# Adding a skip term at PSUM eviction instead of by identity matmuls, and a changed instruction-fetch estimate in a kernel's own ordering pass

## The chip, the cores and the metric

The kernel runs on one core of a Trainium2 chip. The core has five engines that run side by side: TensorE (PE, matrix multiplies; its weight loads are shown apart as PEld), VectorE (DVE), ScalarE (ACT), GpSimd (POOL) and SyncE (SP, which only issues DMAs here). Matmuls read SBUF and write PSUM, which has eight banks; DVE and ACT move results from PSUM to SBUF. The metric is the device time of one execution, in microseconds; lower is better.

## The reference, cut to what matters

The kernel computes a forward pass and all its gradients for a block of a state-space layer (a long convolution, done by FFT) times a gated linear unit, behind one layer norm. S is 2048, D is 512, F is 1376, everything is bfloat16.

```python
def _layernorm(x, axis=-1, eps=1e-5):
    m = jnp.mean(x, axis=axis, keepdims=True)
    v = jnp.var(x, axis=axis, keepdims=True)
    return (x - m) / jnp.sqrt(v + eps)
...
    def _B_ref(x, w_gate, w_up, w_down):
        g = jnp.einsum("bsd,df->bsf", x, w_gate)
        u = jnp.einsum("bsd,df->bsf", x, w_up)
        h = _sigmoid(g) * u
        return jnp.einsum("bsf,fd->bsd", h, w_down)
    x = A_q
    xn = _layernorm(x, axis=-1)
    s = _A_ref(xn, A_k, A_v, A_shift_k, A_ssm_k, A_ssm_D)
    g = _silu(_B_ref(xn, B_w_gate, B_w_up, B_w_down))
    return x + s * g
...
    _out, _vjp = jax.vjp(_f, A_q, A_k, A_v, A_shift_k, A_ssm_k, A_ssm_D, B_w_gate, B_w_up, B_w_down)
    _grads = _vjp(grad_out)
```

Inside `_A_ref`, with xn for q: k is shifted by a short convolution and multiplied by v; the result is convolved along S with `ssm_k` by FFT of length 4096; y is that convolution plus `kv * ssm_D`, and s is `q * y`. The gradient of xn has three parts: through the gate path (dg times w_gate transposed), through the up path (du times w_up transposed), and one that comes past both, straight from `q * y`. The third is the skip term of this document; the kernel calls it `dxa`.

## The kernel before

The kernel does not emit instructions as its Python runs. It records every operation (class `Rec`), and at the end `order` puts them in an order, `emit` writes it out. So every matmul of a burst has line 558 in the profile and every other operation line 560, and it is read by engine, operation and tile shape.

`order` is a list scheduler. It keeps a time at which each engine is free, gives each operation an estimated duration (`cost`, `dcost` for DMAs), chooses PSUM banks, and for an operation recorded by `evac` chooses ACT or DVE. Among the operations that are ready on an engine it takes the lowest number, that is, the one recorded earliest. Its inner function `fetch` (line 386) counts PE instructions, two for each matmul (a weight load and the matmul), in blocks of `IBLK` = 256, and makes PE wait until `IFETCH` = 5.0 us have passed since the last block was begun. If that wait is over 0.3 us for a burst of small array tiles (any mode but "full"), a full-array burst is taken in its place, when one is ready (lines 436 to 439). Line 391 adds nothing: both branches of it are 0.0.

The recorded order comes from generators ("streams") that `run_streams` interleaves. Each has a total of work and a start and end on a common scale, the pair of numbers behind its work; the stream whose place on the scale is lowest goes next. The program has three stages, run as such:

- First stage (to about 190 us): the gate and up projections (`strG`) beside the FFTs of the kernel and of kv (`strK`, `strV`).
- Second stage, `stepB`: eight pairs of token blocks q. For each, `d_gen(q)` (44 matmuls of 256 columns: dg and du), `z_gen(q+1)` (22 matmuls of 512 columns, then eight of 128 for a transposition) and `x_gen(q)` (two tiles t, each one identity matmul and 22 matmuls of 512 columns). In `x_gen` the identity matmul (line 1163) puts `dxa[:, t]` into PSUM; the other 22 accumulate on it. ACT copies the sum to SBUF as `dxn` with a row sum (line 1171), DVE multiplies it with xn with a second row sum (1172), and a short chain through `sm` and `u1` gives the norm's gradient.
- Last stage: `dW` (the three weight gradients, 688 full-array matmuls of up to 512 columns), `frontC` (forward FFT of the upstream gradient, small array tiles of 64x128 and 64x32) and `endC` with `backC` and `taps` (inverse FFTs, tiles of 32x128, 64x64 and 128x32, and the short convolution's gradients). `dW` reads transposed blocks L that SP loads by DMA_TRANSPOSE (`ld_L`, twelve of them, three buffers), `backC` reads spectra KK from DRAM (`ld_KK`). `rec.late` (line 1420) marks the first operation recorded after the second stage's buffers are freed.

What sets the order around the change: PE's, DVE's, ACT's and SP's queues as `order` wrote them, and the stream numbers of lines 1409, 1422 and 1423.

Of the kernel before, what the change touches and what calls it, by code (L numbers as in the profile page):

```python
# [8 lines left out]
ACT = mybir.ActivationFunctionType  # L9
ALU = mybir.AluOpType  # L10
# [14 lines left out]
NFB = 11  # L25
# [137 lines left out]
class Rec:  # L163
# [3 lines left out]

    NEAR = 300
    BUBBLE = 0.12
    IBLK, IFETCH = 256, 5.0  # L170
    late = 1 << 30
    ENGS = ("tensor", "vector", "scalar", "gpsimd", "sync")
    KINDS = {"f4": [(0, 1, 2, 3), (4, 5, 6, 7)], "m2": [(4, 5), (6, 7), (2, 3), (0, 1)],
# [178 lines left out]
    def order(self):  # L352
# [28 lines left out]
        pipe = {"gpsimd": 0.0, "hw": 0.0, "act": 0.0}  # L381
        table = None
        pemode = "full"
        iblk = [0, 0.0]

        def fetch(op, t, occ, commit):
            n = 2 * (len(op.alts[0][2]) if op.alts[0][1] == "burst" else 1)
            k, b = iblk
            wait = 0.0
            if k + n >= self.IBLK:  # L390
                gap = self.IFETCH + (0.0 if op.n >= self.late else 0.0)
                wait = max(0.0, b + gap - (t + occ * (self.IBLK - k) / n))
                b = t + wait + occ * (self.IBLK - k) / n
                k -= self.IBLK
            if commit:
                iblk[:] = [k + n, b]
            return wait
        held = [None] * 8
        seq = []
# [23 lines left out]
        while ndone < len(ops):  # L423
# [29 lines left out]
            t, n, e, shared = best  # L453
            op = ops[n]
# [28 lines left out]
            if op.dma:  # L483
                occ, d = self.dcost(alt)
                me = {"gpsimd": "gpsimd", "scalar": "act"}.get(e, "hw")
                t = max(t, pipe[me] - (30.0 if me == "gpsimd" else 12.0))
# [77 lines left out]
def run_streams(streams, until=None):  # L564

    live = [list(st) + [0.0] * (5 - len(st)) for st in streams]
    while live:
        if until is not None and until():
            break
        for st in sorted(live, key=lambda s: s[2] + (s[3] - s[2]) * s[4] / s[1]):  # L570
            try:
                c = next(st[0])
            except StopIteration:
                live.remove(st)
                break
            if c:
                st[4] += c
                break
        else:
            raise RuntimeError("all streams blocked")  # L580
    return live
# [68 lines left out]
def kernel_impl(ctx, tc, A_q, A_k, A_v, A_shift_k, A_ssm_k, A_ssm_D, B_x, B_w_gate, B_w_up, B_w_down,  # L650
                grad_out, out_0, out_1, out_2, out_3, out_4, out_5, out_6, out_7, out_8, out_9):
    nc = tc.nc
# [29 lines left out]
    ident = Ring(ar, [P]).ap  # L682
# [31 lines left out]
    flags = set()  # L714
# [186 lines left out]
    B = ar.view(B_r.blks[0][0], [2, 2, 32, 2 * 32], bf16).rearrange("p g c j (u w) -> p g c j u w", u=2)  # L901
# [173 lines left out]
    for src, w, wT in ((B_w_gate, wg, wgT), (B_w_up, wu, wuT)):  # L1075
        nc.sync.dma_start_transpose(wT[:, 0:NFB - 1, :], src[:, 0:128 * (NFB - 1)])
        ps = nc.ps("m1", [4, 128], f32)
# [79 lines left out]
    def x_gen(q):  # L1157
        dgT, duT, dxa, goj = T[q]["dg"], T[q]["du"], T[q]["dxa"], T[q]["go"]
        for t in range(2):
            i = 2 * q + t  # L1160
            xn = xnA[:, i, :]
            ps = nc.ps("m1", [D], f32)
            nc.burst("full", 0.216, [("matmul", (ps[:], ident, dxa[:, t]), dict(start=True, stop=False))])
            for srcT, wT, last in ((dgT, wgT, False), (duT, wuT, True)):
                for f0, f1 in ((0, 4), (4, 8), (8, 11)):
                    nc.burst("full", (f1 - f0) * 0.216, [("matmul", (ps[:], srcT[:, fb, 128 * t:128 * t + 128], wT[:, fb, :]),
                             dict(start=False, stop=last and fb == NFB - 1)) for fb in range(f0, f1)])
                    yield (f1 - f0) * 512
            dxn, u1, sm = dxn_r.next(), u1_r.next(), small.next()
            r = rstd_all[:, i:i + 1]  # L1170
            nc.scalar.activation(dxn, ps[:], ACT.Identity, accum_out=sm[:, 0:1])
            nc.vector.scalar_tensor_tensor(u1, dxn, 1.0, xn, ALU.mult, ALU.mult, accum_out=sm[:, 1:2])
            nc.vector.scalar_tensor_tensor(sm[:, 2:4], sm[:, 0:2], -1.0 / D, r.to_broadcast([P, 2]), ALU.mult, ALU.mult)
            nc.scalar.activation(u1, dxn, ACT.Identity, bias=sm[:, 2:3], scale=r)
            nc.vector.scalar_tensor_tensor(u1, xn, sm[:, 3:4], u1, ALU.mult, ALU.add)
            nc.vector.tensor_tensor(goj[:, t], u1, goj[:, t], ALU.add)
        dma2o(nc.sync, o1C[:, :, 2 * q:2 * q + 2, :], goj)
# [45 lines left out]
    def dW():  # L1223
        for n, (s, c) in enumerate(jobs):
            f0, w = CH[s][c]
            while ("L", n) not in stC:
                yield 0
            blk = stC.pop(("L", n))
            L = blk.ap
            nblk = -(-w // 128) if s == 0 else 4  # L1230
            for b in range(nblk):
                acc = nc.ps("hi", [512], f32)
                kf = min(128, w - b * 128) if s == 0 else 128
                wo = D if s == 0 else w
                for j0 in range(0, NJ, 2):
                    calls = []
                    for j in (j0, j0 + 1):
                        kw = dict(start=(j == 0), stop=(j == NJ - 1))
                        if s == 0:
                            calls.append(("matmul", (acc[0:kf, :], L[:, j, b * 128:b * 128 + kf], dzA[:, j, :]), kw))  # L1240
                        else:
                            calls.append(("matmul", (acc[:, 0:w], xnA[:, j, b * 128:(b + 1) * 128], L[:, j, 0:w]), kw))
                    nc.burst("full", 2 * (wo / 2400 + 0.0025), calls)
                    if j0 % 4 == 2 and j0 < 14:
                        yield 4 * wo
                ot = ot_r.next()
                nc.evac(ot[0:kf, 0:wo], acc[0:kf, 0:wo], wo)
                if s == 0:
                    nc.sync.dma_start(out_9[f0 + b * 128:f0 + b * 128 + kf, :], ot[0:kf, :])
                else:  # L1250
                    nc.sync.dma_start((out_7 if s == 1 else out_8)[b * 128:(b + 1) * 128, f0:f0 + w], ot[:, 0:w])
                if b == nblk - 1:
                    Lfree.append(blk)
                    ld_L()
                    if n == 3:
                        stC["v"] = ar.view(dz_r.blks[0][0], [NJ, D], bf16)
                        for j in range(0, NJ, 4):
                            dma2(nc.sync, stC["v"][:, j:j + 4], vC[:, :, j:j + 4])
                yield 4 * wo
# [10 lines left out]
    def frontC():  # L1270
        for n in range(8):
            cg, u = n // 2, n % 2
            c0 = cg * GW + 64 * u
            if u == 0:
                yield from step1n(lambda j: y2A[:, j, c0:c0 + GW])
            U = flip(stA["V"][:, 32 * u:32 * u + 32])
            while stC["nY"] + len(YS_r.aps) <= n:
                yield 0
            Y = YS_r.next()
            step3(U, Y)  # L1280
            stC["Y", n] = Y
            yield 2048
# [82 lines left out]
    def endC():  # L1365
        yield from backC()
        row4, row6 = ot_r.next(), ot_r.next()[:, 0:GW]
        for lag in range(4):
            nc.vector.tensor_copy(skout[:, :, lag:lag + 1], res[:, :, 3 - lag:4 - lag])
        po = nc.ps("m1", [GW, 4], f32)  # L1370
        for t in range(4):
            nc.tensor.matmul(po[0:4, :, t], skout[:, :, t], ident, start=True, stop=True)
        nc.evac(row4[0:4, :], po[0:4].rearrange("p a t -> p (a t)"), 512)
        nc.sync.dma_start(out_4.rearrange("(g p) t -> g (p t)", p=P), row4[0:4, :])
        pd = nc.ps("m1", [GW], f32)
        nc.tensor.matmul(pd[0:4, :], dDo, ident, start=True, stop=True)
        for e in range(2):
            nc.evac(row6[0:4].rearrange("p (u w e) -> p e u w", u=2, e=2)[:, e],
                    pd[0:4].rearrange("p (e u w) -> p e u w", e=2, u=2)[:, e], 64)
        nc.sync.dma_start(out_6.rearrange("(g p) -> g p", p=P), row6[0:4, :])  # L1380

    def gated(g, flag):
        yield from g
        flags.add(flag)
    live = run_streams([(gated(stepB(), "B"), 8 * 45056, 0.0, 1.0)], until=lambda: "d5" in flags)
# [5 lines left out]
    live = run_streams(live, until=lambda: "z15" in flags)  # L1391
# [5 lines left out]
    live = run_streams(live, until=lambda: "d7" in flags)  # L1397
# [8 lines left out]
        ld_KK(m)  # L1406
    YS_r = Ring(ar, [2, 1024], n=2)
    V_r, U_r = Ring(ar, [64, 32, 2]), Ring(ar, [32, 32, 2], n=2)
    live = run_streams(live + [(dW(), 35 * 8192, 0.98, 1.79), (frontC(), 8 * 4096, 0.88, 1.38)], until=lambda: "B" in flags)
    for r in [wgT_r, wuT_r, go_r, dg_r, du_r, dxa_r, dxn_r, u1_r]:  # L1410
        r.free()
    kh = Ring(ar, [NJ + 3, D]).ap
# [6 lines left out]
    dm_r = Ring(ar, [4, 32], f32)  # L1419
    rec.late = len(rec.ops)  # L1420
    dw, fr = live
    live = run_streams([(dw[0], dw[1] - dw[4], 0.0, 1.0), (fr[0], fr[1], -0.02, 0.57, fr[4]),
                        (gated(endC(), "back"), 4 * 20480, -0.03, 0.54)], until=lambda: "back" in flags)
    run_streams(live)
    rec.emit()

# [59 lines left out]
```

## Time and profile before

| | us |
|---|---|
| median of 3 runs | 520.48 (520.48 to 520.87) |
| the profiled execution's own time | 521.04 |
| its span, first to last instruction | 519.3 |
| PE busy | 468.8 (90%) |
| DVE busy | 387.1 (75%) |
| ACT busy | 283.1 (55%) |
| POOL busy | 47.6 (9%) |
| mean granted TensorE clock | 0.975 |
| DMA traffic | 111.23 MB, 214 GB/s |

The profiled execution took 521.04 us, of which 1.74 us lie around the span of 519.3. It was 0.56 us above the median. PE is busy almost without a gap from 188 us to 368 us; after that, to 498 us, it has gaps. Busy times of matmuls overlap each other, so a busy PE is not PE at its peak: where PE's pace matters, count how many matmuls go by in a stretch and divide. "issue" in a wait means that the profile shows nothing that the engine waited for.

### The profile page before, as it was taken

The numbers are of one execution on the slowest core, as the hardware profiler recorded it, in microseconds if no ns is written. First come the engines' busy times: TensorE is split into PE (matmuls) and PEld (weight loads), VectorE is DVE, ScalarE is ACT, GpSimd is POOL, SyncE is SP. The second block draws the span as 40 slices with busy tenths as digits, with TensorE's granted clock in tenths as the row PEclk, the third lists the DMA queues.
The fourth block names the chain that finished last, engine by engine and source line by source line (L and its number), as shares of the span: only waits on it lengthen the run. The fifth ranks groups of instructions, "written<-read, shape, count | busy, mean of one in ns | idle before, by whom it ended". The sixth has DMA issues, their size and how long they took to land.

```text
span 519.3 us, 14659 instructions
## 1 busy us (share of the span) xinstructions
PE 468.8 (90%) x6388; PEld 303.4 (58%) x6417; DVE 387.1 (75%) x622; ACT 283.1 (55%) x361; POOL 47.6 (9%) x83
## 2 busy tenths in 40 slices
PE   3899898999899789999999999999867979978995
PEld 3687666777676464556556556444434546646664
DVE  8569988767787895877878778576781699963880
ACT  5557787766875743544454446746653764344111
POOL 5023232121121000000000001000000000000000
PEclk9999999999989999999999999999998989979999
DMA  8998697754849969875865947999999996937866
GB/s 218 252 306 207 232 233 207 215 199 172 264 137 265 224 181 281 245 190 159 249 162 178 256 136 181 234 278 261 280 187 222 247 281 149 235 92 174 176 201 202
DMA packets 162360, 111.23 MB, mean 214 GB/s; under 512 B 102389, under 2 KB 145369, under 8 KB 162296
## 3 DMA queue, kind: packets, MB, share of 16 engines
q1 hardware_dynamic: 154104, 86.49, 68.9%
q0 software_dynamic: 6080, 22.75, 13.0%
q10 hardware_dynamic: 2112, 1.05, 0.8%
q8 instruction: 50, 0.82, 0.6%
q14 instruction: 14, 0.11, 0.1%
HBM read 38.44 MB, written 46.83 MB: 164 GB/s over the span
## 4 chain that ended last, share of the span: by engine, by line
PE 59%; issue 15%; DVE 11%; ACT 7%; DMA 5%; SPq 2%; POOL 0%; DVEq 0%; POOLq 0%; ACTq 0%
PE psum L558 59%; DVE slab L560 11%; ACT slab L560 7%; DMA slab<-slab 2%; SPq L560 2%; DMA slab<-in_A_q_dram 1%; DMA slab<-in_A_v_dram 1%; PE psum L560 0%; POOL slab L560 0%; DVEq L560 0%; POOLq L560 0%; ACTq L560 0%
## 5 line engine op out<-in xcount | busy, mean ns | idle before, releaser
L558 PE MATMUL psum<-slab 32*128 32x64 bf16 (+10 forms) x6379 | 467.1, 260 | 45.0 <-ACT slab L560 18.8
L558 PEld LDWEIGHTS <-slab 128*128 128x128 bf16 (+5 forms) x6408 | 302.7, 102 | 208.8 <-issue 64.7
L560 ACT CAST slab<-psum 128x1024 bf16<-128x1024 f32 (+5 forms) x265 | 221.0, 887 | 162.8 <-PE psum L558 133.3
L560 DVE TENSOR_TENSOR slab<-slab 128x1024 bf16<-128x1024 bf16 (+5 forms) x327 | 242.4, 790 | 42.1 <-PE psum L558 23.4
L560 ACT ACTIVATE slab<-psum 128x1024 bf16<-128x1024 f32 (+2 forms) x60 | 49.8, 835 | 63.1 <-PE psum L558 60.3
L560 DVE CAST slab<-psum 128x1024 bf16<-128x1024 f32 (+3 forms) x27 | 31.0, 1149 | 43.5 <-PE psum L558 23.8
L560 DVE STREAM_TRANSPOSE slab<-slab 128x512 f32<-128x512 f32 x48 | 31.0, 685 | 6.1 <-ACT slab L560 6.0
L560 DVE TENSOR_TENSOR slab<-psum,slab 128x1024 bf16<-128x1024 f32 (+2 forms) x28 | 28.1, 1003 | 8.1 <-PE psum L558 7.5
L560 DVE SCALAR_TENSOR_TENSOR slab<-slab 128x512 bf16<-128x512 bf16 (+1 forms) x48 | 24.8, 528 | 11.3 <-ACT slab L560 11.1
L560 DVE TENSOR_SCALAR slab<-slab 128x1 f32<-128x1 f32 (+9 forms) x63 | 20.5, 364 | 4.1 <-PE psum L558 1.8
L560 POOL DMA_DIRECT2D slab<-slab x8 | 4.3, 541 | 176.6 <-DVE slab L560 176.6
L560 ACT ACTIVATE slab<-slab 128x512 bf16<-128x512 bf16 (+2 forms) x18 | 15.7, 872 | 2.6 <-DVE slab L560 1.3
L560 POOL MEMSET slab<- 128x128 bf16 (+3 forms) x7 | 3.3, 480 | 148.0 <-PE psum L558 144.9
L560 POOL DMA_DIRECT2D KK_d<-slab x16 | 9.0, 563 | 67.1 <-ACT slab L560 52.7
L560 POOL TENSOR_TENSOR slab<-slab 128x1 f32<-128x1 f32 (+1 forms) x20 | 11.3, 574 | 24.9 <-DVE slab L560 22.8
L560 DVE BATCH_NORM_STATS2 slab<-slab 128x6 f32<-128x512 bf16 x16 | 10.5, 672 | 0.8 <-DMA slab<-in_A_q_dram 0.8
L560 POOL DMA_DIRECT2D hS_d<-slab x8 | 8.8, 1097 | 12.7 <-DVE slab L560 6.3
L560 DVE COPY slab<-slab 128x1216 bf16<-128x1216 bf16 (+2 forms) x16 | 7.1, 465 | 0.7 <-ACT slab L560 0.7
L560 POOL DMA_DIRECT2D sF_d<-slab x6 | 3.3, 555 | 10.8 <-ACT slab L560 10.8
L560 ACT ACT_TABLE_LOAD x2 | 2.6, 1283 | 2.9 <-issue 2.9
L560 ACT ACTIVATION_READ_ACCUMULATOR slab<-psum 128x1 f32 x16 | 3.1, 196 | 0.0
L560 POOL DMA_DIRECT2D ksh_d<-slab x4 | 2.2, 562 | 6.7 <-ACT slab L560 6.7
(16 smaller groups left out, 15.8 us busy)
## 6 DMA issues: line engine op xcount, KB each, us to landing
KK_d<-slab POOLq DMA_DIRECT2D x16, 512.0 KB, 5.0
slab<-KK_d SPq DMA_DIRECT2D x16, 512.0 KB, 5.2
out_dram<-slab SPq DMA_DIRECT2D x58, 128.0 KB, 2.9
hS_d<-slab POOLq DMA_DIRECT2D x8, 704.0 KB, 6.2
dgS_d<-slab SPq DMA_DIRECT2D x8, 704.0 KB, 4.1
duS_d<-slab SPq DMA_DIRECT2D x8, 704.0 KB, 7.0
sF_d<-slab POOLq DMA_DIRECT2D x6, 704.0 KB, 4.4
slab<-sF_d SPq DMA_DIRECT2D x6, 704.0 KB, 8.1
```

The lines of the kernel that those rows point to most:

```text
L558: getattr(self.nc.tensor, m)(*[place(v) for v in aa], **{x: place(v) for x, v in kk.items()})
L560: getattr(getattr(self.nc, eng), meth)(*[place(v) for v in a], **{x: place(v) for x, v in k.items()})
```

## The change

There are two edits and the numbers that go with the second.

In `x_gen` the identity matmul is left out, so the first of the 22 matmuls starts the accumulation. ACT's copy with a row sum is replaced by one DVE operation that reads PSUM, adds `dxa[:, t]`, writes `dxn` and gives the same row sum.

In `order`, `IFETCH` becomes a pair. For operations from `rec.late` on, when a new block is begun, the gap to the next one is taken as 6.0 us if the estimated end of the queue of hardware DMAs lies more than 3 us behind the block's begin, else as 4.2 us; before `rec.late` it stays 5.0. The numbers of the three last-stage streams change too: both streams that begin beside the second stage, and `frontC` and `endC` after it.

```diff
-    IBLK, IFETCH = 256, 5.0
+    IBLK, IFETCH = 256, (4.2, 6.0)
...
-        iblk = [0, 0.0]
+        iblk = [0, 0.0, self.IFETCH[0]]
...
-            k, b = iblk
+            k, b, gap = iblk
             wait = 0.0
             if k + n >= self.IBLK:
-                gap = self.IFETCH + (0.0 if op.n >= self.late else 0.0)
                 wait = max(0.0, b + gap - (t + occ * (self.IBLK - k) / n))
                 b = t + wait + occ * (self.IBLK - k) / n
                 k -= self.IBLK
+                gap = 5.0 if op.n < self.late else self.IFETCH[pipe["hw"] > b + 3.0]
             if commit:
-                iblk[:] = [k + n, b]
+                iblk[:] = [k + n, b, gap]
...
-            nc.burst("full", 0.216, [("matmul", (ps[:], ident, dxa[:, t]), dict(start=True, stop=False))])
...
-                             dict(start=False, stop=last and fb == NFB - 1)) for fb in range(f0, f1)])
+                             dict(start=not last and fb == 0, stop=last and fb == NFB - 1)) for fb in range(f0, f1)])
...
-            nc.scalar.activation(dxn, ps[:], ACT.Identity, accum_out=sm[:, 0:1])
+            nc.vector.scalar_tensor_tensor(dxn, ps[:], 1.0, dxa[:, t], ALU.mult, ALU.add, accum_out=sm[:, 0:1])
...
-    live = run_streams(live + [(dW(), 35 * 8192, 0.98, 1.79), (frontC(), 8 * 4096, 0.88, 1.38)], until=lambda: "B" in flags)
+    live = run_streams(live + [(dW(), 35 * 8192, 0.93, 1.64), (frontC(), 8 * 4096, 0.87, 1.54)], until=lambda: "B" in flags)
...
-    live = run_streams([(dw[0], dw[1] - dw[4], 0.0, 1.0), (fr[0], fr[1], -0.02, 0.57, fr[4]),
-                        (gated(endC(), "back"), 4 * 20480, -0.03, 0.54)], until=lambda: "back" in flags)
+    live = run_streams([(dw[0], dw[1] - dw[4], 0.0, 1.0), (fr[0], fr[1], -0.09, 0.53, fr[4]),
+                        (gated(endC(), "back"), 4 * 20480, 0.0, 0.63)], until=lambda: "back" in flags)
```

The built program has 6401 matmuls instead of 6417. Its order is the same up to the first `x_gen`; in the second stage it differs by the edit alone, and from the stage's last pair on every queue is in another order.

## The prediction

> **What bounds the kernel now.** I read the page's busy times first, then the chain of work that ended last, then PE's timeline and busy times by stretch. In the second stage the chain is PE alone:
>
> ```profile
> PE 468.8 (90%) x6388; PEld 303.4 (58%) x6417; DVE 387.1 (75%) x622; ACT 283.1 (55%) x361; POOL 47.6 (9%) x83
> ...
> 202.92 10.74 PE psum L558 x49
> ...
> 213.71 9.08 PE psum L558 x69
> ...
> 222.85 10.74 PE psum L558 x49
> ```
>
> One pair q takes 19.93 us (202.92 to 222.85), all of it PE. The busy times of such a period, and of 8 us in it that hold only 512-column matmuls (columns: stretch, its length, then busy us and count of PE, PEld, DVE, ACT, POOL, the granted clock, DMA share, GB/s):
>
> ```profile
> 231.10:250.90 19.80, 19.70 (x119) 11.35 (x120) 16.07 (x30) 9.51 (x14) 0.00 (x0) 1.00 0.69 198
> 247.50:255.50 8.00, 7.95 (x37) 3.60 (x37) 7.63 (x13) 3.33 (x5) 0.00 (x0) 1.00 1.02 297
> ```
>
> 37 matmuls in 8.00 us are 0.216 us each; DVE has 3.7 us free in a period, ACT 10.3. In the last stage PE has gaps (PE's timeline; in brackets the idle time before a row and what ended it):
>
> ```profile
> 371.11 1.01 PE L558 MATMUL psum<-slab 32*128 32x64 bf16 x72 [1.43 <-DVE slab L560]
> ...
> 387.56 4.66 PE L558 MATMUL psum<-slab 128*128 128x512 bf16 x104 [3.03 <-issue]
> ...
> 400.68 16.22 PE L558 MATMUL psum<-slab 64*64 64x128 bf16 x270 [3.63 <-issue]
> ...
> 420.96 22.28 PE L558 MATMUL psum<-slab 128*32 128x128 bf16 x382 [2.28 <-DVE slab L560]
> ...
> 458.56 1.26 PE L558 MATMUL psum<-slab 32*128 32x64 bf16 x125 [1.85 <-DVE slab L560]
> 461.27 7.62 PE L558 MATMUL psum<-slab 128*128 128x320 bf16 x122 [1.45 <-ACT slab L560]
> ```
>
> With 0.66, 0.46, 0.52, 0.83 and 0.90 (issue) more in the same view, waits for DVE or ACT cost 9.5 us and "issue" 7.6. From 498 us to its end at 514.0 PE runs leftover dW matmuls; then one eviction and the last stores fill the span to 519.3. So every us that PE saves or loses anywhere after 190 us moves the end by one us.
>
> **Identity matmuls: -3.5 us.** 16 x 0.216, in a stage where nothing else sets the pace. ACT loses 0.600 us and the 0.196 of reading its sum for each tile, DVE gains one operation. Rows of the nearest kinds:
>
> ```profile
> L560 DVE SCALAR_TENSOR_TENSOR slab<-slab 128x512 bf16<-128x512 bf16 x32 | 22.4, 717 | 11.2 <-ACT slab L560 11.1
> L560 DVE TENSOR_TENSOR slab<-psum,slab 128x768 bf16<-128x768 f32 x8 | 7.6, 952 | 4.2 <-PE psum L558 4.2
> L560 DVE CAST slab<-psum 128x512 bf16<-128x512 f32 x1 | 0.7, 690 | 0.1
> ```
>
> The trace has no such operation on PSUM: from below 0.69 (the copy), from above 0.95 (two operands, but 768 columns), plus 0.08 for reading the sum. I take 0.83 with it, by the same operation in SBUF. Two a period make DVE 16.07 + 1.66 = 17.7 us busy in a period of 19.93 - 0.43 = 19.50. That is hidden as long as DVE's chain fits. Walked from the end of z's matmuls: hT (1.6) and nine products end at 7.6, the first tile's sum is ready on PE at 4.8, so its eviction waits for nothing; the second tile ends on PE at 10.0 and DVE comes to it at 10.6. Queued behind it are the product with xn, dg and du of the same pair, and 1-sig of the next; dg and du are done by about 17.7, and the next x_gen needs them at 19.5. The transposition needs z's chain after 37 matmuls (8.0 us) and has it at about 5. The tile's PSUM bank is held until 8.4 instead of 5.6 us, and two evictions later PE asks for banks at 10.0. So cost zero, cover 1.8 us a period; were the cover gone, each us over is paid seven times.
>
> **Last stage, waits for DVE and ACT: -4.1.** I laid the orders of the two built programs side by side. For each PE instruction that waits for DVE or ACT I set the PE work since the matmul that feeds the awaited operation against that engine's operations in the same stretch, at the rows' durations. In the old order the tap matmuls have 2.72 us of PE work against 4.98 on DVE, short by 2.26: the trace shows 2.28. All shortfalls of the old order add to 5.8 where the trace has 9.5; those of the new one to 3.3 (1.4 at a 32x128 burst early on, 1.0 at another, four small ones; the tap matmuls no longer wait). Scaled alike, 5.4. Bounds: -6.2 unscaled, 0 if backlog on DVE comes back elsewhere. SP's queue moves too: the eight loads of v, two KK loads and a ksh load now stand right behind a DMA_TRANSPOSE; at 0.55 us an issue after its 9.8 us, v lands some 20 us later, and PE has 18.6 us of work and several fetch waits before it needs it. KK loads have 16 us or more. POOL's few halo copies (0.54 us each) have 16 us and more as well. I give these no cost; the bound above holds it.
>
> **Last stage, instruction fetch: +4.7.** The page lists queue "q8 instruction: 50, 0.82" (packets, MB): 16 KB each, against 12,847 PE instructions, so one packet for 256. The three "issue" gaps lie before PE's instructions 8644, 9156 and 11972, which are 2 and 11 times 256 apart. In the trace a packet starts 0.4 to 4.6 us after PE enters the block before, takes 1 us, and PE goes on no sooner than 1.45 us after it has landed. From one entry to the next it took 7.2 us (380.3 to 387.6) and 6.6 (394.1 to 400.7) while a DMA_TRANSPOSE ran, 4.6 without (470.3 to 474.9). Now the work in each block: 0.216 us for 512 columns, 0.150 for 352, 0.62 for a burst of 64 small 32x128 tiles, 1.0 for 64 of 64x64 or 128x32. The old order's shortest are 2.3, 2.5, 2.6, 3.1, 3.3 and 3.3 us, several covered by other waits. The new one has seven blocks under 4.4: 3.8, 2.9, 3.5 (4.4 with its 1.0 wait), 4.3, 3.4, 1.8, 3.8, together 24.4 us, one run of four of them beside two transposes that now follow each other on SP. At a mean price p of 5.2 (two of seven at 6.5, the others between 3.6 and 5.5) they take 36.4, so 12.0 us of waiting, 12.3 with one small wait near the end; less 7.6 is 4.7. Bounds: p = 4.0 gives 3.9, thus -3.7; p = 6.5 gives 21.1, thus +13.5.
>
> [...]
>
> **Last stage, half clock: -2.5.** Gaps cost twice (busy times as above):
>
> ```profile
> 384.49:387.90 3.41, 0.38 (x3) 0.21 (x3) 3.38 (x6) 1.17 (x2) 0.00 (x0) 1.00 1.29 167
> 387.90:391.31 3.41, 3.41 (x48) 1.29 (x49) 0.64 (x2) 0.00 (x0) 0.00 (x0) 0.50 0.98 236
> ...
> 456.17:459.58 3.41, 1.56 (x130) 1.19 (x129) 2.62 (x6) 2.01 (x3) 0.00 (x0) 1.00 0.10 27
> 459.58:463.00 3.42, 1.97 (x31) 1.18 (x19) 3.35 (x5) 3.42 (x4) 0.00 (x0) 0.50 0.68 161
> ```
>
> After a 3.41-us stretch with PE idle for half or more, the next runs at clock 0.50. The last stage has five such stretches, each worth up to 1.7 us: 8.5. The new order's waits fall mostly on short blocks, where slow work hides under the next fetch; I count four stretches, one of them half hidden: 6.0. Bounds -5 and +3.4. [...]
>
> **Sum.** -3.5 - 4.1 + 4.7 - 2.5 = -5.4. The profiled execution's span 519.3 becomes 513.9, with the 1.74 around it 515.6; that execution was 0.56 above the median: 515.1, I say 515.
>
> **Rivals.**
> 1. Only the matmuls pay, the rest cancels: 517.0. For it: the work in the last stage is the same, and what fetch loses is about what DVE gains. Against: the shortfalls reproduced the old trace's largest wait to 0.02 us. It needs the three last-stage terms to add to about 0.
> 2. Slower, by starved fetch: four short blocks in a row under two transposes. With p = 6.5 the term is +13.5, the sum +3.4, so 524. It decides from p = 6.0 on, where the sum crosses zero (7 x 6.0 - 24.4 + 0.3 = 17.9, less 7.6 is 10.3, against -10.1). For it: two observed blocks at 6.6 and 7.2. Against: both had a transpose in flight over the whole block, and only two or three of the seven do.
> 3. DVE becomes the second stage's bound: if the new operation costs 0.95 + 0.08 and its waits for ACT open another 1.5 us, each of seven periods grows by some 0.6: +4.2, so 519. Against: 1.8 us of cover.
> 4. Fetch stays hidden, each next block there in time: -3.5 - 4.1 - 2.5, no gain from the 7.6 counted, 510.4; with that too, lower still. Against it stand the short blocks. [...]
>
> **How the numbers follow.** The forecast 0.52, rivals 0.20, 0.17, 0.06, 0.05. A change under 0.2% (1.04 us) can't be told from none here. Faster takes the forecast, most of rival 1 and all of 4: 0.75. Same takes the edges of 1 and 3, 0.07; slower 0.18, rival 2 and a little of 3. The likeliest case alone spans 510 to 518; reaching rival 4's edge and into the lighter half of rival 2, 509.5 to 521.5.
>
> **What would show it.** In the changed profile the period should be 19.5 us with DVE near 17.7 busy and PE without gaps to about 360; the new DVE row near 0.75. The tap matmuls' 2.28 should be gone. "issue" gaps should sit at short blocks beside transposes and add to about 12 us, with four half-clock stretches. A period over 19.6, gaps for DVE over 8 us, or "issue" over 18 us would make it wrong.

## The result, and the profile after

Timed together, the changed kernel took 523.89 us (520.39 to 529.26, 20 runs) and the kernel before 519.34 (518.17 to 521.88, 20 runs). The ratio is 1.0088, interval 1.0065 to 1.011: about 4.6 us slower. The forecast was 515.0 with a range up to 521.5. The profiled execution took 526.38 us, its span is 524.6. Where some executions of a kernel took over 1.5% more than its fastest, the ratios below leave these out.

The second stage came out as forecast. From the page of after (busy times; then a group of instructions: busy us, mean ns of one, idle time before):

```profile
PE 466.6 (89%) x6401; PEld 301.7 (58%) x6401; DVE 397.5 (76%) x656; ACT 272.7 (52%) x327; POOL 47.2 (9%) x83
...
L560 DVE SCALAR_TENSOR_TENSOR slab<-psum,slab 128x512 bf16<-128x512 f32 x16 | 11.0, 690 | 5.2 <-PE psum L558 5.2
```

One period in after, busy times by stretch (columns as before: stretch, length, busy us and count of PE, PEld, DVE, ACT, POOL, clock, DMA share, GB/s):

```profile
211.30:230.70 19.40, 19.40 (x120) 11.15 (x118) 17.18 (x34) 8.12 (x11) 0.00 (x0) 1.00 0.65 188
```

The new operation takes 0.69 us, and PE has no gap. The loss lies behind the stage. PE's timeline of after (start, length; in brackets the idle time before the row and what ended it):

```profile
366.69 8.21 PE L558 MATMUL psum<-slab 128*128 128x512 bf16 x116 [3.44 <-ACT slab L560]
...
378.27 11.87 PE L558 MATMUL psum<-slab 64*64 64x64 bf16 x198 [1.20 <-issue]
...
393.68 9.04 PE L558 MATMUL psum<-slab 128*128 128x352 bf16 x234 [2.04 <-DVE slab L560]
405.01 5.03 PE L558 MATMUL psum<-slab 64*64 64x64 bf16 x128 [2.29 <-issue]
411.75 3.91 PE L558 MATMUL psum<-slab 64*64 64x128 bf16 x48 [1.71 <-issue]
...
422.87 12.42 PE L558 MATMUL psum<-slab 32*128 32x64 bf16 x149 [1.41 <-issue]
...
450.94 8.60 PE L558 MATMUL psum<-slab 32*128 32x64 bf16 x281 [1.53 <-DVE slab L560]
462.17 10.27 PE L558 MATMUL psum<-slab 32*128 32x64 bf16 x211 [2.63 <-issue]
```

The first tap matmuls' wait of 2.28 us is gone, as forecast; the second ones now wait 0.80 (at 436.09). But counting every gap of 0.3 us or more after 340 us, waits for DVE and ACT add to 12.15 us (before: 9.48) and "issue" to 10.39 (before: 7.56). DVE itself waits for loads more than it did. Before had one such row:

```profile
347.40 3.88 DVE L560 TENSOR_TENSOR slab<-slab 128x2048 bf16<-128x2048 bf16 x5 [3.14 <-DMA slab<-KK_d]
```

After has four, 7.93 us in all (the one not shown, of 1.08 us for KK, is at 348.01). DVE's timeline of after:

```profile
365.39 6.04 DVE L560 TENSOR_TENSOR slab<-slab 128x2048 bf16<-128x2048 bf16 x9 [2.10 <-DMA slab<-KK_d]
...
394.89 7.42 DVE L560 TENSOR_TENSOR slab<-slab 128x2048 bf16<-128x2048 bf16 x10 [1.26 <-DMA slab<-KK_d]
...
417.15 1.23 DVE L560 TENSOR_TENSOR slab<-slab 128x2048 bf16<-128x2048 bf16 x1 [3.49 <-DMA slab<-KK_d]
```

ACT's timeline of after, just ahead of PE's largest gap:

```profile
366.06 4.93 ACT L560 CAST slab<-psum 128x512 bf16<-128x512 f32 x6 [2.12 <-DMA out_dram<-slab]
```

ACT can't copy a dW bank out because the store that empties its buffer has not landed, so PE gets no bank and waits 3.44 us. (ACT had such a wait in before too, of 3.31 us at 455.97.) SP's queue of after at that place (start, time the issue took):

```profile
355.02 0.54 SPq L560 DMA_DIRECT2D slab<-KK_d  x1
356.99 2.21 SPq L560 DMA_DIRECT2D out_dram<-slab  x3
359.76 10.78 SPq L560 DMA_TRANSPOSE slab<-dgS_d  x1
370.63 1.18 SPq L560 DMA_DIRECT2D slab<-in_A_k_dram  x2
371.90 0.54 SPq L560 DMA_DIRECT2D slab<-KK_d  x1
...
382.92 6.54 SPq L560 DMA_TRANSPOSE slab<-dgS_d  x1
389.55 1.00 SPq L560 DMA_DIRECT2D slab<-KK_d  x2
```

The stores were issued just ahead of a DMA_TRANSPOSE and landed at about 366, some 8.5 us later (their median on the page is 3.5). KK loads are late in two ways. The one issued at 355.02 stood ahead of the DMA_TRANSPOSE and took 10.3 us to land, at 365.37, where DVE waited for it. The one issued at 389.55 stood behind a DMA_TRANSPOSE, went out as soon as SP was free and took 5.2 us; DVE waited until 394.89. The third wait shown, 3.49 us, is put down to KK by the profile, but it is for v: the operation is the taps' product with v, it waits for the semaphores of all eight loads of v, and the last of these, issued at 407.57 behind the next DMA_TRANSPOSE, landed at 417.03. So KK makes 4.44 us of the 7.93 and v 3.49. In the last stage four stretches of 3.41 us ran at half clock, as counted; two of them:

```profile
394.55:397.96 3.41, 3.41 (x65) 1.96 (x51) 3.04 (x4) 2.84 (x3) 0.00 (x0) 0.50 1.17 196
404.79:408.20 3.41, 3.19 (x33) 1.55 (x34) 1.37 (x3) 2.02 (x2) 0.00 (x0) 0.50 1.09 305
```

Last, PE ends at 517.05 and the span at 524.6: 7.6 us of tail, where before had 513.99 and 5.3. The first stage, the same program, ended 1.77 us later than in the profile of before (189.53 against 187.76; the other profiles here, k1's aside, have 187.9 to 189.4), which is the run and not the change.

### The profile page after: what moved, and what is told of

It reads as the page before. It is cut to its first block, busy times and chain, and to the rows that moved or that the text cites. A ratio compares the mean times of both kernels' runs of the same rounds, so it can differ in the third digit from the quotient of the medians.

```text
span 524.6 us, 14678 instructions
## 1 busy us (share of the span) xinstructions
PE 466.6 (89%) x6401; PEld 301.7 (58%) x6401; DVE 397.5 (76%) x656; ACT 272.7 (52%) x327; POOL 47.2 (9%) x83
## 2 busy tenths in 40 slices
DMA packets 162360, 111.23 MB, mean 212 GB/s; under 512 B 102389, under 2 KB 145369, under 8 KB 162296
## 3 DMA queue, kind: packets, MB, share of 16 engines
q1 hardware_dynamic: 154104, 86.49, 70.3%
## 4 chain that ended last, share of the span: by engine, by line
PE 53%; issue 16%; DVE 13%; ACT 8%; DMA 7%; SPq 1%; POOL 0%; DVEq 0%; ACTq 0%; POOLq 0%
PE psum L558 53%; DVE slab L560 13%; ACT slab L560 8%; DMA slab<-in_A_v_dram 2%; DMA out_dram<-slab 2%; DMA slab<-in_A_q_dram 2%; SPq L560 1%; DMA slab<-slab 1%; DMA slab<-KK_d 1%; PE psum L560 0%; POOL slab L560 0%; ACT L560 0%; DVEq L560 0%; ACTq L560 0%; POOLq L560 0%
## 5 line engine op out<-in xcount | busy, mean ns | idle before, releaser
L560 ACT CAST slab<-psum 128x1024 bf16<-128x1024 f32 (+6 forms) x263 | 220.4, 889 | 193.9 <-PE psum L558 172.1
L560 ACT ACTIVATE slab<-psum 128x1024 bf16<-128x1024 f32 (+2 forms) x44 | 40.2, 917 | 40.1 <-PE psum L558 37.2
L560 DVE SCALAR_TENSOR_TENSOR slab<-psum,slab 128x512 bf16<-128x512 f32 x16 | 11.0, 690 | 5.2 <-PE psum L558 5.2
```

The source lines that it names most:

```text
L560: getattr(getattr(self.nc, eng), meth)(*[place(v) for v in a], **{x: place(v) for x, v in k.items()})
```

## The experiments

All ratios are to the kernel before, timed in the same job; 1% is 5.2 us. To change one thing and keep every queue's order, the kernels got a field `sub`: the operation is ordered as it was, and something else is written out in its place.

```diff
-                eng, meth, a, k = op.alts[q]
+                eng, meth, a, k = op.alts[q] if op.sub is None else op.sub
```

### Edit or order?

p1 keeps the order of before and makes the eviction edit; p2 does so with a one-column matmul in the place of each identity matmul. p3 keeps the order of after and puts the identity matmul and ACT's copy back. e1 makes the eviction edit in the source of before and lets the order be laid anew by the old rule and numbers.

```diff
 # p1, in x_gen of before
-            nc.burst("full", 0.216, [("matmul", (ps[:], ident, dxa[:, t]), dict(start=True, stop=False))])
+            nc.burst("full", 0.216, [("matmul", (ps[:], ident, dxa[:, t]), dict(start=True, stop=False))]).sub = ("tensor", "burst", [], {})
...
-            nc.scalar.activation(dxn, ps[:], ACT.Identity, accum_out=sm[:, 0:1])
+            nc.scalar.activation(dxn, ps[:], ACT.Identity, accum_out=sm[:, 0:1]).sub = (
+                "vector", "scalar_tensor_tensor", (dxn, ps[:], 1.0, dxa[:, t], ALU.mult, ALU.add), dict(accum_out=sm[:, 0:1]))
```

```diff
 # p2, in the place of the empty burst
+                "tensor", "burst", [("matmul", (ps[:, 0:1], ident, dxa[:, t, 0:1]), dict(start=True, stop=True))], {})
 # p3, in x_gen of after
+                    skip = [("matmul", (ps[:], ident, dxa[:, t]), dict(start=True, stop=False))] if not last and f0 == 0 else []
+                    nc.burst("full", (f1 - f0) * 0.216, mms(not last)).sub = ("tensor", "burst", skip + mms(False), {})
...
+            nc.vector.scalar_tensor_tensor(dxn, ps[:], 1.0, dxa[:, t], ALU.mult, ALU.add, accum_out=sm[:, 0:1]).sub = (
+                "scalar", "activation", (dxn, ps[:], ACT.Identity), dict(accum_out=sm[:, 0:1]))
 # e1, in x_gen of before
-            nc.burst("full", 0.216, [("matmul", (ps[:], ident, dxa[:, t]), dict(start=True, stop=False))])
...
-            nc.scalar.activation(dxn, ps[:], ACT.Identity, accum_out=sm[:, 0:1])
+            nc.vector.scalar_tensor_tensor(dxn, ps[:], 1.0, dxa[:, t], ALU.mult, ALU.add, accum_out=sm[:, 0:1])
```

> The order of the kernel before, operation by operation, with the eviction edit alone: the 16 identity matmuls are left out where they stood and the DVE operation stands where ACT's copy stood. Theory 1 (the eviction gains, the new last-stage order loses): 16 x 0.216 us, so 3.5 us faster than before, 515.8, give or take 1.5 because all later fetch blocks begin 32 instructions earlier in the work; second-stage period 19.5 us. Theory 2 (the DVE eviction itself costs, by its bank held longer or by DVE's backlog): no faster than before, up to 4 us slower, with PE gaps for DVE in the second stage.

> As p1, but in the place of each identity matmul stands one of a single column, which the next matmul overwrites, so that every later instruction stands in the same place of its fetch block as in the kernel before. Theory 1: 16 x (0.216 - 0.06) gained, 2.5 us faster than before, 516.8. If p1 is off by more than 1.5 us from its forecast and p2 is not, the place of the blocks' boundaries is what made the difference. Theory 2: as p1.

> The order of the changed kernel, operation by operation, with the identity matmul put back before each tile's first matmul and ACT's copy in the place of the DVE operation. Theory 1: the new order alone, so 3.5 us slower than the changed kernel: 8 us slower than before, 527. Theory 2: the order costs nothing, 519 to 520, as before.

> The eviction edit in the source alone; the ordering pass keeps its fetch gap of 5.0 us and the old stream numbers, and makes a last-stage order of its own, which is neither the old nor the new one. Theory 1: second stage 3.5 us shorter, the last stage anywhere within 5 us of the old one: 511 to 521, likeliest 516. Theory 2: slower than before.

Measured: p1 1.0038 (1.0004 to 1.0071), p2 1.0078 (1.0047 to 1.0109), p3 1.0108 (1.0067 to 1.015), e1 1.0096 (1.0061 to 1.0132). The new order alone loses as much as the whole change, though less than the 8 us expected, and so does another new order (e1, outside its 511 to 521). But p1 and p2 miss the question. PE's timeline of p2:

```profile
255.55 19.72 PE L559 MATMUL psum<-slab 128*128 128x128 bf16 x120 [0.32 <-DVE slab L561]
```

DVE's eviction stands in DVE's queue where ACT's copy stood in the common order, and PE waits 0.32 us for it each period. p4 writes it out just ahead of the operation that first reads its result, and is p1 otherwise; p5 is p4 with the one-column matmuls; p4r is p4 again.

```diff
+                if op.sub is not None and op.sub[0] == "vector":
+                    late[op.n + 1] = (op, q)
+                    continue
+                if op.n in late:
+                    order.append(late.pop(op.n))
+                order.append((op, q))
```

> The order of before on every queue, with the eviction edit alone: no identity matmuls, and VectorE's eviction put in its own queue just ahead of the operation that first reads it, so that PE no longer waits 0.32 us a period for it as in p1 and p2. Theory 1 (the eviction edit is a gain, the new order of the last stage is the loss): the period is 19.5 us instead of 19.93, the matmuls' 3.5 us come through, and the time is 2.5 to 4.5 us below that of before, 0.9915 to 0.995 of it. Theory 2 (taking the matmuls out costs in the last stage what it saves, since the blocks of instruction fetch shift by 32 instructions against the work): period 19.5 as well, but 0.998 to 1.005. Theory 3 (VectorE has no room for it): period over 19.7 and rows of PE that wait for VectorE in the second stage.

> As p4 (order of before, eviction edit, VectorE's eviction just ahead of its first reader), with a matmul of one column in the place of each identity matmul, so that the blocks of 256 instructions lie against the work as in before. If the shift by 32 instructions costs something in p4, this is faster than p4 by it less 16 one-column matmuls of at most 0.07 us: 0.990 to 0.995 of before against p4's 0.9937. If the shift is worth nothing, 0.994 to 0.997. If the shift is a gain in p4, up to 0.999.

> p4 once more, for more undisturbed runs of it. If the eviction edit alone is a gain in the old order, 0.990 to 0.997 of before, as p4 had; if p5 tells what it is worth beside the transposing loads, 0.998 to 1.005.

Measured: p4 0.9937 (0.989 to 0.9984), p4r 0.9944 (0.9908 to 0.9981), p5 1.0037 (1.0007 to 1.0066). In the old order the eviction edit is a gain of 2.9 us (p4r). p5 is a miss that stays open: its sixteen matmuls, 0.03 us each by the period (19.55 us against p4r's 19.49), explain 0.5 us of the 4.8 between it and p4r. The gain isn't whole. DVE's timeline of p4r (this execution took 522.66 us, the median is 517.79):

```profile
346.56 3.88 DVE L570 TENSOR_TENSOR slab<-slab 128x2048 bf16<-128x2048 bf16 x5 [4.50 <-DMA slab<-KK_d]
364.64 4.84 DVE L570 TENSOR_TENSOR slab<-slab 128x2048 bf16<-128x2048 bf16 x7 [3.62 <-DMA slab<-KK_d]
```

The reader is to see the first row: DVE is ready for KK at 342.06 here (346.56 less 4.50) and at 344.26 in before, 2.2 us earlier; the wait ends at 346.56 here and at 347.40 in before, only 0.8 us earlier.

### Is the order of before a special one?

s1 is the kernel before with one number changed.

```diff
-    live = run_streams(live + [(dW(), 35 * 8192, 0.98, 1.79), (frontC(), 8 * 4096, 0.88, 1.38)], until=lambda: "B" in flags)
+    live = run_streams(live + [(dW(), 35 * 8192, 0.97, 1.79), (frontC(), 8 * 4096, 0.88, 1.38)], until=lambda: "B" in flags)
```

> The kernel before with one number changed: the start of dW's stream 0.97 instead of 0.98. Nothing is computed otherwise; the recorded order of the last stage differs. Theory 1 (the order of before is an unusually good one among many alike, so that nearly any other recorded order loses a few us): 2 to 6 us slower than before, 1.004 to 1.012. Theory 2 (only the new fetch estimate and the new numbers make the bad order): within 1 us of before.

Measured 1.0099 (1.0063 to 1.0135): as bad as after, without anything of the change. PE's timeline of s1:

```profile
363.38 15.03 PE L558 MATMUL psum<-slab 64*32 64x512 bf16 x158 [3.18 <-issue]
398.62 7.36 PE L558 MATMUL psum<-slab 128*128 128x352 bf16 x128 [3.12 <-issue]
```

Its waits for DVE and ACT add to 4.0 us only, its "issue" gaps to 13.7. So another order trades one for the other and loses all the same. e1, p3 and s1, three orders other than that of before, all lie at 1.0096 to 1.0108.

### Are late loads of KK the cause?

k1 has the order of after, with the loads of KK from the fourth on issued by GpSimd; k2 has them issued by ScalarE.

```diff
-            nc.sync.dma_start(stC["KK", m], KK_d[m // 2, :, m % 2].rearrange("p (c x) -> p c x", c=2))
+            src = KK_d[m // 2, :, m % 2].rearrange("p (c x) -> p c x", c=2)
+            op = nc.sync.dma_start(stC["KK", m], src)
+            if m >= 3:
+                op.sub = ("gpsimd", "dma_start", (stC["KK", m], src), {})
```

> The order of after, with the loads of KK from the fourth on issued by GpSimd's queue instead of SP's. Theory 1 (they come late because they stand behind a DMA_TRANSPOSE that holds SP's queue): the waits of VectorE for KK_d at about 365, 395 and 417 us (2.10, 1.26 and 3.49 us) go, PE's gaps after them shrink, and the time is 2 to 4 us below that of after, 0.992 to 0.996 of it. Theory 2 (the transfers themselves are late, because the DMA engines are busy with the transpose): the loads are issued earlier but land as late, the waits stay within 0.5 us, and the time is within 1 us of after's. Theory 3 (VectorE's waits are off the path): the waits go, and the time is still within 1 us.

> The order of after, with the loads of KK from the fourth on issued by ScalarE's queue, where an issue took 0.34 us in t1, and not by GpSimd's, where k1 found them to land after a median of 14.3 us. Theory 1 (KK is late because SP's queue is held): VectorE's waits for KK_d of 2.10, 1.26 and 3.49 us go, and the time is 1.5 to 4 us below after's, 0.992 to 0.997 of it. Theory 2 (the DMA engines are busy with the transpose, whichever queue asks): loads issued earlier land as late, the waits stay, the time is within 1 us of after's, or above it where ScalarE waits for a free buffer.

k1 measured 1.0336 (1.0291 to 1.0382), outside all its theories. The page of k1, DMA issues (KB each, median us from issue to landing):

```profile
slab<-KK_d POOLq DMA_DIRECT2D x13, 512.0 KB, 14.3
```

The same loads took 6.0 in after. (The profiled execution of k1 took 559.65 us; the median behind its ratio is 538.99.) k1 tells nothing on SP's queue: the cure was worse. k2 measured 1.0061 (1.0037 to 1.0086), 1.4 us below after's ratio with intervals that overlap. No row of DVE waits for KK any more. The wait for v, 3.49 in after, is still there with 2.02; DVE's timeline of k2:

```profile
412.08 1.23 DVE L561 TENSOR_TENSOR slab<-slab 128x2048 bf16<-128x2048 bf16 x1 [2.02 <-DMA slab<-in_A_v_dram]
```

Waits for DVE and ACT are 10.6 us (after 12.2), "issue" 10.4 as in after. p6 is p4, and bk is the kernel before, with all loads of KK but the first on ScalarE's queue (the edit of k2 with `m >= 1`).

> p4 with all loads of KK but the first issued by ScalarE's queue instead of SP's. If it is SP's held queue that eats the second stage's gain, VectorE's waits for KK_d at 347 and 365 us (5.15 and 2.61 us in p4, 5.31 and 4.25 in p5) go, and the time is 4 to 7 us below before, 0.987 to 0.993 of it, below both kernels. If the DMA engines are the limit, the loads land as late, other waits for DMAs take their place, and it is 0.994 to 1.004.

> The kernel before with all loads of KK but the first issued by ScalarE's queue. VectorE's wait of 3.14 us for KK_d at 347 us goes. As PE has work beside it there, theory 1 (the wait was covered in before) has the time within 1 us of before; theory 2 (it was on the path) has it 2 to 3 us below, 0.994 to 0.996. p6 divided by this is what the eviction edit is worth once KK isn't late: 0.992 to 0.994 if its 3.5 us come through.

p6 measured 1.0007 (0.9971 to 1.0042), bk 1.0072 (1.005 to 1.0094): both worse than without the move, and bk outside both its theories; why, no view here shows. In p6 the first load, left on SP, was the late one (DVE waits 5.17 us for it). KK alone isn't the cause.

### Are the transposing loads the cause?

na is after, nb before and np4 is p4, each with the twelve transposing loads of L emitted as ordinary loads of as many bytes, at the same places in the queue. The three weight gradients of dW are then products with untransposed data.

```diff
-            nc.sync.dma_start_transpose(blk.ap[:, :, 0:w], srcs[s][f0:f0 + w, :])
+            op = nc.sync.dma_start_transpose(blk.ap[:, :, 0:w], srcs[s][f0:f0 + w, :])
+            flat = srcs[s][f0:f0 + w, :].rearrange("f s -> (f s)").rearrange("(p j x) -> p j x", p=128, j=NJ)
+            op.sub = ("sync", "dma_start", (blk.ap[:, :, 0:w], flat), {})
```

> The order of after on every queue, with the twelve transposing loads of dW's blocks L emitted as ordinary loads of as many bytes, one contiguous piece a partition, so that SP's queue isn't held for 5 to 11 us at a time and the DMA engines are less busy; the weight gradients then are products with untransposed data, everything else is computed as before. To be set against nb, the same for before. Theory A (the forecast failed because loads and stores stand late behind DMA_TRANSPOSE on SP, and fetches beside it): with the transposes gone the new order is faster than the old one, as its own terms said: 0.985 to 0.993 of nb. Theory B (the loss is in the order itself, its waits between PE, VectorE and ScalarE and its fetch blocks): still slower than nb, 1.004 to 1.015 of it, as after is of before. Between, 0.995 to 1.003 of nb: part of each. Waits of VectorE for KK_d should be below 0.5 us in all by both.

> The order of before, with the same twelve transposing loads emitted as ordinary loads. It is the other half of the pair with na. By both theories it gains what the fetches gain, since the 3.03 and 3.63 us gaps of before lie beside a transpose: 2 to 6 us below before, 0.988 to 0.996 of it. If it gains nothing, transposes in flight weren't what made those two fetches slow.

> p4 (order of before, eviction edit alone, VectorE's eviction just ahead of its first reader) with the twelve transposing loads of L emitted as ordinary loads of as many bytes, so that the weight gradients are products with untransposed data. If the second stage's 3.5 us are lost to the transposing loads in p5, they come through here: 3 to 4.5 us below nb, 0.989 to 0.992 of before. If they are lost for another reason, within 1.5 us of nb: 0.995 to 1.001 of before.

| order, eviction | transposing loads | ordinary loads |
|---|---|---|
| old, old | 1 | nb 0.9978 (0.9954 to 1.0001) |
| old, new | p4r 0.9944 (0.9908 to 0.9981) | np4 0.9844 (0.9815 to 0.9873) |
| new, old | p3 1.0108 (1.0067 to 1.015) | |
| new, new | after 1.0088 (1.0065 to 1.011) | na 0.9892 (0.9865 to 0.9919) |

With ordinary loads the whole change is a gain: na is 0.9914 of nb, 4.5 us. With transposing loads it is a loss of 4.6. Against the old order with the same eviction, the new order costs 7.5 us beside transposing loads (1.0088 to 0.9944) and 2.5 without (0.9892 to 0.9844). The difference, 5.0 us, is what the new order pays for standing beside transposing loads; the intervals leave it uncertain by some 3 us, and the 2.5 by some 2. Read along the rows, the transposing loads cost 1.1 us in before, less than nb's expectation, 5.2 in p4r and 10.2 in after. np4's gain on nb, 7.0 us, is more than was expected of it. The DMA view of the stretch from 340 to 440 us shows what they take, in before:

```profile
DMA packets 40335, 23.85 MB, mean 239 GB/s; under 512 B 34815, under 2 KB 37087, under 8 KB 40319
...
q1 hardware_dynamic: 40255, 23.51, 100.4%
```

In after:

```profile
q1 hardware_dynamic: 39831, 22.92, 102.8%
```

And in na:

```profile
DMA packets 15300, 23.06 MB, mean 231 GB/s; under 512 B 1104, under 2 KB 11824, under 8 KB 15088
...
q1 hardware_dynamic: 15156, 22.62, 76.9%
```

(Packets, MB, time of the packets as a share of the 16 engines'. A share over 100% means that packet times overlap on an engine, so it is no exact measure of how full an engine is.) About as many bytes, but with transposes the packets book all 16 engines for these 100 us (100.4% in before, 102.8% in after), and most are small (34,815 of before's 40,335 under 512 B). The loads of KK land no faster in na, though: they have a median of 6.0 us from issue to landing on both pages. DVE has no wait for KK left in na, and 0.08 us for v, whose last load is issued at 398.94 and lands at 405.60; both go with an earlier issue as well. About the same megabytes cost 26 points more of the engines' time with the transposing loads (after's 102.8% against na's 76.9%).

### The held queue or the busy engines?

x1 (after) and x2 (p4) issue each transposing load in four pieces, with SP's next DMA between two pieces as long as nobody reads the block. By a held queue I mean that SP is busy issuing one DMA and its next one goes out only after it: in after the DMA_TRANSPOSE of 359.76 took SP 10.78 us, and the next load went out at 370.63.

```diff
+            part = [("sync", "dma_start_transpose", (blk.ap[:, j:j + 4, 0:w], srcs[s][f0:f0 + w, 128 * j:128 * j + 512]), {})
+                    for j in range(0, NJ, 4)]
+            op.sub, op.more = part[0], part[1:]
```

> The order of after, with each of the twelve transposing loads of L issued in four pieces of four token blocks, and SP's next DMA between two pieces, as long as nobody reads the block. Theory 1 (it is SP's held queue): a hold is at most 3 us, loads of KK and stores are issued some 5 us earlier, and the time is 2 to 5 us below after's, 0.998 to 1.004 of before. Theory 2 (the DMA engines are busy with the same bytes): within 1 us of after's, 1.006 to 1.011.

> p4 with the transposing loads in four pieces in the same way. Theory 1: 2 to 5 us below p4r, 0.984 to 0.991 of before, below both kernels. Theory 2: within 1 us of p4r.

SP's queue of x1, at the place shown of after:

```profile
359.64 2.20 SPq L565 DMA_TRANSPOSE slab<-dgS_d  x1
364.69 0.51 SPq L565 DMA_DIRECT2D slab<-in_A_k_dram  x1
365.29 1.40 SPq L568 DMA_TRANSPOSE slab<-dgS_d  x1
...
369.21 0.57 SPq L565 DMA_DIRECT2D slab<-KK_d  x1
```

The hold of 10.78 us is now pieces of 1.4 to 2.2 (the longest of any piece from 340 to 420 us is 3.1, and one just ahead took 4.0). x1 measured 1.01 (1.0047 to 1.0154) against after's 1.0088, x2 0.9947 (0.9924 to 0.9971) against p4r's 0.9944: no difference. x1's view of 340 to 440 us still has q1 at 104.2%; its DVE (the last row is the product with v again, though the profile names a store):

```profile
364.33 6.04 DVE L565 TENSOR_TENSOR slab<-slab 128x2048 bf16<-128x2048 bf16 x9 [3.25 <-DMA slab<-KK_d]
...
419.68 1.22 DVE L565 TENSOR_TENSOR slab<-slab 128x2048 bf16<-128x2048 bf16 x1 [9.60 <-DMA out_dram<-slab]
```

So shorter holds alone gain nothing. But they did not leave everything as it was: "issue" gaps of PE fell to 4.2 us in x1 (10.4 in after) and 3.0 in x2 (7.9 in p4r), while waits for DVE and ACT rose to 19.5 (12.2) and 14.2 (12.1). Nor is SP's queue ruled out: the pieces that x1 issues from 340 to 440 us hold it for 41.1 us in all, the whole ones of after for 45.0, and the KK load shown goes out only 1.0 us earlier (369.21 against 371.90, counted from the end of the first stage). The loads of v, between the pieces now, go out 4.5 us later counted so (the last at 410.39 against 407.57), and DVE's wait for them grew from 3.49 to 9.60. Ordinary loads take away both the holds (na's issues of them at 356.55, 377.93 and 385.17 took SP 0.57, 0.56 and 0.33 us) and the small packets (1,104 under 512 B in na's view above, 34,519 in after's); which of the two costs the time, no run tells apart. x2 and p4 are also the versions that beat both kernels: the eviction edit alone, with the order of before.

### The tail

t1 is after, with the stores of dW's last two jobs issued by ScalarE.

```diff
-                    nc.sync.dma_start((out_7 if s == 1 else out_8)[b * 128:(b + 1) * 128, f0:f0 + w], ot[:, 0:w])
+                    dst = (out_7 if s == 1 else out_8)[b * 128:(b + 1) * 128, f0:f0 + w]
+                    op = nc.sync.dma_start(dst, ot[:, 0:w])
+                    if n >= 10:
+                        op.sub = ("scalar", "dma_start", (dst, ot[:, 0:w]), {})
```

> The order of after, with the stores of the last two jobs of dW issued by ACT's queue instead of SP's. Theory 1 (the 2.3 us by which after's tail, from PE's end to the span's end, is longer are SP's queue: the last store is issued late behind the stores of the taps): the tail goes from 7.6 us to about 5.3, the time 1.5 to 2.5 us below after's. Theory 2 (the DMA engines have a backlog at the end): the last store is issued earlier and lands as late, tail 7 us or more, time within 0.7 us of after's.

Measured 1.0069 (1.0033 to 1.0105) and a tail of 6.3 us: between the theories, and not told apart from after. The tail goes with the order and not with the transposes: 7.7 us in na, 5.2 in nb, 5.3 in np4. After's last taps end later, so that 25 stores stand in SP's queue from 501.52 on, where before has 20 from 499.48.

## Why the prediction was wrong

**The step that failed** is the term "waits for DVE and ACT", and in it the sentence "I give these no cost" on SP's moved loads, with its grounds, 18.6 us of PE's work until v is needed and 16 us or more for KK. The term was put at -4.1 and measured +2.7, outside its bounds (-6.2 to 0). The moved loads did make an engine wait: in after DVE waited 3.49 us for v and 4.44 for KK, in before 3.14 for KK and nothing for v, and in na, with ordinary loads in the place of the transposing ones, 0.08 for v and nothing for KK. The grounds set issue times against PE's work; it was DVE that needed v first, for the taps' product, and none of them asked when a load lands that is issued beside or behind a transposing load. From 340 to 440 us the DMA engines were booked at 100.4% in before already, and the page's row of DMA shares shows nines up to 428 us (40 slices of 13 us, the share of each in tenths):

```profile
DMA  8998697754849969875865947999999996937866
```

The forecast drew nothing from that row. na and nb show that the transposing loads decide the sign: with ordinary loads in the same queues, the change is a gain of 4.5 us.

**Identity matmuls, -3.5:** right. The period is 19.5 us, DVE 17.2 busy in it (17.7 forecast), the operation 0.69 (0.75). The edit alone is worth 2.9 us in the old order and 7 without transposing loads (np4 against nb). Seven is twice what the matmuls are worth; np4 has one half-clock stretch and nb three, which at up to 1.7 us each would be the rest, but this is not tested.

**Waits for DVE and ACT, -4.1:** missed by 6.8 us. Of these, 2.8 go with the transposing loads. The other 4.0 are the count itself: without transposing loads the waits are 9.50 in na and 9.58 in nb, no gain at all. The tap's 2.28 went, but where the two largest waits of the count were 1.4 and 1.0, those of na are 2.06 and 1.53, and smaller ones (1.38, 0.88, 0.66 and less) fill the rest. Scaling a count that saw 5.8 of 9.5 us was no cure for what it did not see.

**Instruction fetch, +4.7:** right in kind, +2.8 measured (10.4 us, forecast 12.3). In na it is 5.5 us, in nb 6.0: without transposing loads the new order has no more "issue" waits than the old one, so the whole +2.8 goes with them. Rival 4, with fetch hidden, did not come about: "issue" gaps cost PE 10.4 us in after, and 13.7 in s1. Two readings of the working were off: the fetch of 4.6 us "without" a transposing load had one that was issued at 465.73 and landed at 474.5, and behind it PE went on 1.31 us after the packet had landed, not 1.45. The bound at p = 4.0 also lets blocks of 4.4 and 4.3 us count as negative waits; without that it is 4.6 instead of 3.9. None of it moves the forecast of 515.

**Half clock, -2.5:** four stretches as counted. In the 3.41 us just ahead of them PE was busy for 0.55, 1.37, 1.34 and 0.78 us. Ahead of the five in before it was busy for 0.38, 0.87, 1.13, 1.56 and 1.97, so the working's "idle for half or more" does not hold for the fifth. At up to 1.7 us each (half of 3.41) that is 6.8 against 8.5, so -1.7; whether one of them was half hidden, the profile doesn't show.

**The tail:** "every us that PE saves or loses anywhere after 190 us moves the end by one us" did not hold; the order added 2.3 us behind PE's end.

The measured terms, from one profiled execution of each kernel, add to -3.5 + 2.7 + 2.8 - 1.7 + 2.3 = +2.6. With the first stage's 1.8 that is 4.4 of the 5.3 us between the profiled spans. The other 0.9 is not accounted for, and it is rather 2.5, since ten "issue" gaps of 0.16 us, below the 0.3 counted here, are in before and not in after. Rival 2 had the side right and the cause wrong: "issue" stayed at 10.4 us, far from the 17.9 at which it decides. The second sign named for a wrong forecast, gaps for DVE over 8 us, was not quite met at 7.9; ACT's 4.2 came on top. Rival 3's price does not follow from its parts: 16.07 + 2 x 1.03 + 1.5 = 19.63 against 19.50 is 0.1 us a period and not 0.6. It did not come about either.

**Open:** whether SP's held queue or the engines' time is what the transposing loads cost; and why before pays 1.1 us for them, p4r 5.2 and after 10.2 (e1 and s1 were not run with ordinary loads). That the order of before was picked from many by its time would fit s1, but no run shows it. Open too are the 4.0 us that the count of waits missed, p5, and which of the tail's stores counts.

## What to carry to other kernels

Read the DMA share by stretch before costing a moved transfer: where all 16 engines are booked (100.4% here) and the queue is held (10.78 us by one load here), don't put it at nothing, but set its landing against the need. When an edit comes with a newly laid order, run the edit with the old order pinned, and the new order without the edit; here one gained 0.6% and the other lost 1.1%. One order of a list scheduler is one draw: here, moving one stream's start by a hundredth cost 1%.

## What the runs showed of the hardware that was not expected

With the twelve transposing loads the page counts 162,360 packets, with ordinary ones 109,176, and the hardware queue takes 70.3% of the engines over the span of after against 61.1% in na, at 86.49 MB both. Loads of 512 KB issued by GpSimd landed after a median of 14.3 us, against 6.0 from SP, in the same order (k1's profiled execution, of 559.65 us); six "issue" gaps of PE there were 3.5 to 6.5 us long. PE's "issue" gap near 400 us reached 6.12 us in p6, where before has 3.63. Splitting the transposing loads cut PE's "issue" gaps by 6.2 us in x1 and 4.9 in x2, and won no time (1.01 against after's 1.0088, 0.9947 against p4r's 0.9944).
